# Sigmoid attention and two feed-forward layers on one core: GpSimd's additions and subtractions of weights and unit tiles are done by DVE and ACT

## The chip, the core and the metric

The kernel runs on one core of a Trainium2 chip. The core has a matrix engine (TensorE; in the rows PE, and PEld for its weight loads), VectorE (DVE), ScalarE (ACT), GpSimd (POOL), and SyncE (SP), which here issues nearly all transfers. Each engine works through its own instruction list in order; engines wait for each other on semaphores. The metric is device time in microseconds for one execution: the median of 3 runs of the kernel before is 1112.79 us (1111.52 to 1113.42).

## The reference

```python
# attention: 4 batches, 12 heads, 448 tokens, head size 64
scores = scale * q @ k.T - log(448)
attn = sigmoid(scores);  x = attn @ v            # -> [1792, 768]
# first layer, 1536 wide
xn = x / sqrt(mean(x * x) + 1e-6) * rms_g
g = xn @ w_gate;  val = xn @ w_val
x = (g * sigmoid(g) * val) @ w_out               # -> [1792, 768]
# second layer, 2048 wide
h = x @ w_in
out = (h - tanh(h)) @ w_out2                     # -> [1792, 768]
```

The weight matrices come as 64-bit numbers; everything else, and the result, is 32-bit.

## The kernel before, in words

All activations are kept transposed, in "unit" tiles of 128 x 448 (128 features of one batch's 448 tokens); there are 74 unit buffers. The products of both layers keep 32-bit accuracy by splitting each operand into a high part (a cast to fp32r, line 279) and a low part (the value less its high part: line 350 for weights, 595 and 635 for unit tiles); each product is then three matmuls (high by high, high by low, low by high).

The attention comes first, batch by batch. Then the two batches (0, 1) go through both layers, then the batches (2, 3). A layer has two kinds of jobs, and the jobs take turns:

- Jobs "Ag", "Av" (gate and value) and "C" (the second layer's input matrix) compute 2 x 2 blocks with seven products instead of eight (`seven_units`, matmuls on line 734). For that they need sums and differences of weight blocks (`total`, line 385) and of unit tiles (`right_sum`, line 600), each split again. Two or three products share one PSUM bank, and between them the bank is copied (line 279) or added to an earlier tile (`plus`, line 708). The next product in that bank can't start before that read. Behind them stand SiLU (678), the product of gate and value (681), tanh (685) and the subtraction (686); `parts` splits the results (279 and 635).
- Jobs "B" and "D" (the two output matrices) are ordinary products, six matmuls to a 128 x 128 weight block (line 769). Partial sums go to DRAM and come back.

Weights are prepared two jobs ahead (`conv`): for batches (0, 1) a 64-bit block is loaded, made into 32-bit values (`values32`: a cast on line 279 and one DVE instruction on line 339), summed (385), split (279 and 350), and the 32-bit values are written to DRAM (370); for batches (2, 3) they are read back (419) and split again.

The order of the instructions isn't written by hand. Each operation is given to `Plan.add` with the engines that can do it, a cost in nanoseconds for each, and a mark whether it uses the port that DVE and GpSimd share. `Plan.issue` then goes through the work with a clock for each engine: it takes, for each piece of work that is ready, the engine on which it starts soonest, and among the pieces that can start within 300 ns of the soonest the one that stands first in the program. The result is the fixed order on every engine. The costs are built by small functions: `act(n)`, `dve(n)`, `pool(n)` return a dictionary with one engine, and an operation that has a choice merges them, as on line 350:

```python
add({**dve(n, psum=False), **pool(n)}, lambda e: ENG[e].tensor_sub(lo(), of(), hi().bitcast(F32)), ...)
```

`pool(n)` is offered on lines 350 (low parts of weights), 385 (sums of weights), 538, 541 and 542 (squares for the norm, and their sum; there ACT or DVE took all of them), 595, 600 and 635 (unit tiles), and through line 675 on 681 and 686. The power on line 560 is given to GpSimd alone, with its own cost.

Of the kernel before, what the change touches and what calls it, by code (L numbers as in the profile page):

```python
# [214 lines left out]
def tile_sigmoid_attention_moe_moe(  # L215
# [37 lines left out]
    def slot(kind, pool, shape, dt, tag):  # L253
        return Slot(kind, lambda: pool.tile(shape, dt, tag=tag, name=tag))
# [18 lines left out]
        return {"DVE": ((150 if psum or fast else 210) + n / 0.96 / (2 if fast else 1), fast or (two and not psum))}  # L273

    def pool(n):
        return {"POOL": (230 + n * 2.16, True)}

    def copy(engines, to, of, reads, writes):
        add(engines, lambda e: (nc.scalar.copy if e == "ACT" else nc.vector.tensor_copy)(to(), of()), reads, writes)  # L279
# [68 lines left out]
    def split(n, hi, lo, of, reads, kh, kl):  # L348
        copy({**act(n), **dve(n, fast=True)}, hi, of, reads, [*kh])
        add({**dve(n, psum=False), **pool(n)}, lambda e: ENG[e].tensor_sub(lo(), of(), hi().bitcast(F32)), [*reads, *kh], [*kl])  # L350
# [21 lines left out]
    def conv(j):  # L372
# [11 lines left out]
        def total(to, n, x, y, sub=True):  # L384
            add({**dve(NH, psum=False), **pool(NH)}, lambda e: (ENG[e].tensor_sub if sub else ENG[e].tensor_add)(
                one_of(to.tile, n), one_of(x[0].tile, x[1]), one_of(y[0].tile, y[1])), [x[0][x[1]], y[0][y[1]]], [to[n]])
# [471 lines left out]
    for j in range(len(jobs)):  # L858
# [14 lines left out]
        if seven or tight == 1:  # L873
            n = 6 if seven else 2
# [75 lines left out]
```

## Time and profile before

| | |
|---|---|
| median of 3 runs | 1112.79 us |
| the profiled execution | 1111.01 us |
| its span, first to last instruction | 1109.2 us |
| TensorE busy | 1092.8 us (99%) |
| DVE busy | 701.0 us (63%), 1075 instructions |
| ACT busy | 503.2 us (45%), 896 instructions |
| GpSimd busy | 149.6 us (13%), 108 instructions |
| granted TensorE clock | 1.0 throughout |

The profiled execution took 1.8 us more than its span, which lies around the first and last instruction. It is itself 1.78 us below the median. Of the 108 instructions of GpSimd, 96 are the additions, subtractions and products of lines 350, 385, 595, 600, 635, 681 and 686, four are the powers of line 560, and the rest set constants. Busy time of the matmuls is modelled at their ends: a matmul's record is longer than the distance to the next one's start.

### The profile page before, as it was taken

To read this page: it belongs to the slowest core of one execution; us is meant where nothing else is said; L and a number is where in the kernel's file an instruction comes from. 1 tells how busy PE (TensorE), PEld (TensorE's weight loads), DVE (VectorE), ACT (ScalarE), POOL (GpSimd) and SP (SyncE) were. 2 spreads that over 40 slices of the span, in tenths; PEclk is the share of its full clock that TensorE was granted. 3 is DMA by queue.
4 is the path that set the end of the run, shared out by engine and by line. 5 is a ranking of instruction groups with operands and counts; after the bars stand their busy time and mean duration, and the time that the engine had idled before them with its cause. 6 is when DMAs were issued, how large, how long until landed. Compare 5 with 4: busy or idle time off the path is not lost.

```text
span 1109.2 us, 14723 instructions
## 1 busy us (share of the span) xinstructions
PE 1092.8 (99%) x5364; PEld 914.3 (82%) x5364; DVE 701.0 (63%) x1075; ACT 503.2 (45%) x896; POOL 149.6 (13%) x108
## 2 busy tenths in 40 slices
PE   9999999999999998999999999999999999999998
PEld 3333338999999997999998888999899989999997
DVE  0353816877478789767698966633666686474651
ACT  5776864443255346355364533312344353243431
POOL 0000003300021000123132001200021021222100
PEclk9999999999999999999999999999999999999999
DMA  5774554469668546599899563334344135656432
GB/s 163 246 221 114 143 177 179 146 253 316 212 207 282 208 157 232 181 321 364 288 345 320 192 198 119 115 121 135 103 164 147 57 103 159 195 179 199 146 116 100
DMA packets 92456, 211.40 MB, mean 191 GB/s; under 512 B 25312, under 2 KB 58080, under 8 KB 92384
## 3 DMA queue, kind: packets, MB, share of 16 engines
q1 hardware_dynamic: 92080, 210.30, 56.3%
q8 instruction: 42, 0.69, 0.3%
q14 instruction: 30, 0.25, 0.1%
q10 hardware_dynamic: 304, 0.16, 0.1%
HBM read 137.68 MB, written 72.74 MB: 190 GB/s over the span
## 4 chain that ended last, share of the span: by engine, by line
PE 94%; DVE 4%; issue 1%; ACT 1%; DMA 0%; POOL 0%; DVEq 0%; ACTq 0%; POOLq 0%
PE ps L734 42%; PE ps L769 37%; PE ps L490 7%; PE ps L520 7%; DVE unit L279 1%; DVE wt L350 1%; DVE unit L635 1%; PE ps L286 1%; DVE unit L708 0%; ACT unit L279 0%; DVE unit L681 0%; PE ps L554 0%; DMA wC<-cv 0%; ACT wt L279 0%; DVE unit L600 0%
## 5 line engine op out<-in xcount | busy, mean ns | idle before, releaser
L734 PE MATMUL ps<-unit,wt 128*128 128x448 f32 x2520 | 521.5, 366 | 9.6 <-DVE unit L708 5.4
L734 PEld LDWEIGHTS ps<-unit,wt 128*128 128x128 f32 x2520 | 471.4, 188 | 55.7 <-DVE unit L708 6.9
L769 PE MATMUL ps<-unit,wt 128*128 128x448 f32 x2016 | 413.9, 365 | 1.1 <-ACT wt L279 1.1
L769 PEld LDWEIGHTS ps<-unit,wt 128*128 128x128 f32 x2016 | 378.1, 188 | 33.1 <-ACT wt L279 1.5
L279 ACT COPY unit<-ps 128x448 f32<-128x448 f32 x172 | 91.2, 534 | 329.0 <-PE ps L769 200.5
L279 DVE COPY unit<-ps 128x448 f32<-128x448 f32 x80 | 49.9, 624 | 129.8 <-PE ps L769 124.0
L350 DVE TENSOR_TENSOR wt<-cv,wt 128x768 fp32r<-128x768 f32 (+1 forms) x111 | 101.7, 924 | 18.8 <-ACT wt L279 17.4
L279 ACT CAST wt<-cv 128x768 fp32r<-128x768 f32 (+1 forms) x97 | 75.1, 781 | 41.4 <-PE ps L734 16.3
L497 ACT ACTIVATE unit<-ps 128x448 f32<-128x448 f32 (+1 forms) x192 | 86.5, 547 | 5.9 <-PE ps L490 5.9
L635 DVE TENSOR_TENSOR unit<-unit 128x448 fp32r<-128x448 f32 x94 | 75.8, 807 | 7.4 <-ACT unit L279 4.7
L490 PE MATMUL ps<-wt 64*128 64x448 f32 (+1 forms) x384 | 78.9, 547 | 0.0
L520 PE MATMUL ps<-unit,vs 128*64 128x448 f32 (+1 forms) x384 | 77.7, 545 | 0.0
L350 POOL TENSOR_TENSOR wt<-cv,wt 128x768 fp32r<-128x768 f32 (+1 forms) x25 | 48.2, 1928 | 214.9 <-ACT wt L279 145.5
L708 DVE TENSOR_TENSOR unit<-ps,unit 128x448 f32<-128x448 f32 x84 | 51.9, 619 | 33.2 <-PE ps L734 23.7
L350 POOL TENSOR_TENSOR wt<-wt 128x768 fp32r<-128x768 f32 (+1 forms) x21 | 36.3, 1732 | 269.6 <-ACT wt L279 188.9
L279 ACT CAST wt<-wt 128x768 fp32r<-128x768 f32 (+1 forms) x60 | 44.8, 753 | 53.8 <-PE ps L734 38.0
L339 DVE SCALAR_TENSOR_TENSOR cv<-wt,zero 128x768 uint32<-128x768 uint32 x68 | 66.8, 982 | 2.5 <-ACT unit L535 0.7
L490 PEld LDWEIGHTS ps<-wt 64*128 64x128 f32 (+1 forms) x384 | 32.3, 173 | 43.3 <-issue 36.1
L520 PEld LDWEIGHTS ps<-unit,vs 128*64 128x64 f32 (+1 forms) x384 | 25.2, 136 | 49.1 <-issue 32.9
L279 ACT CAST zero<-wt 128x768 f16<-128x768 bf16 x49 | 53.1, 1083 | 26.6 <-DVE cv L339 19.8
L279 ACT CAST unit<-unit 128x448 fp32r<-128x448 f32 x91 | 51.3, 567 | 25.4 <-DVE unit L681 9.0
L350 DVE TENSOR_TENSOR wt<-wt 128x768 fp32r<-128x768 f32 (+1 forms) x59 | 51.4, 879 | 6.4 <-ACT wt L279 5.5
(49 smaller groups left out, 548.9 us busy)
## 6 DMA issues: line engine op xcount, KB each, us to landing
wt<-in_w_out SPq DMA_DIRECT2D x28, 768.0 KB, 5.9
sumD<-unit SPq DMA_DIRECT2D x72, 224.0 KB, 2.7
unit<-sumD SPq DMA_DIRECT2D x72, 224.0 KB, 4.7
wt<-in_w_in SPq DMA_DIRECT2D x16, 768.0 KB, 5.8
wC<-cv SPq DMA_DIRECT2D x32, 384.0 KB, 4.3
wt<-wC SPq DMA_DIRECT2D x16, 768.0 KB, 4.3
wt<-in_w_gate SPq DMA_DIRECT2D x12, 768.0 KB, 5.2
wt<-in_w_val SPq DMA_DIRECT2D x12, 768.0 KB, 5.4
```

What stands on the lines that cost most here:

```text
L279: add(engines, lambda e: (nc.scalar.copy if e == "ACT" else nc.vector.tensor_copy)(to(), of()), reads, writes)
L286: nc.tensor.matmul(ps[:, :S], lhsT=mark[:, :P], rhs=mark, start=True, stop=True)
L339: add(dve(NW, psum=False), lambda e: nc.vector.scalar_tensor_tensor(out=c.tile.bitcast(U32), in0=r.tile[:, :NW, 1], scalar=13, in1=z.tile, ...
L350: add({**dve(n, psum=False), **pool(n)}, lambda e: ENG[e].tensor_sub(lo(), of(), hi().bitcast(F32)), [*reads, *kh], [*kl])
L490: nc.tensor.matmul(ps[i, c].tile[:n, :S], lhsT=t.tile[rows, at:at + n], rhs=t.tile[rows, :S], start=True, stop=True)
L497: add(act(S, psum=True), lambda e: nc.scalar.activation(to.tile[at:at + n, :S], ps.tile[:n, :S], AF.Sigmoid, bias=-math.log(S), scale=1.0 ...
L520: nc.tensor.matmul(ps.tile[i * D:(i + 1) * D, :S], lhsT=v.tile[:n, c, i, :], rhs=a[c][i].tile[:n, :], start=(c == 0), stop=(c == 3))
L635: add({**pool(S), **dve(S, psum=False)}, lambda e: ENG[e].tensor_sub(c["l"].tile, t.tile, c["h"].tile.bitcast(F32)), [t["t"], kh], [kl])
L708: add(dve(S), lambda e: nc.vector.tensor_add(t.tile, ps.tile[:, :S], t.tile), [ps["t"], t["t"]], [t["t"]])
L734: nc.tensor.matmul(ps.tile[:, :S], lhsT=part(a), rhs=x[b].tile, start=n in ((1, 2, 5) if opening else (1, 5)) and i == 0 and q == 0, stop= ...
L769: nc.tensor.matmul(ps.tile[:, :S], lhsT=wt, rhs=a[p].tile, start=first and i == 0 and k < GR[ph], stop=last and i == 2, skip_group_check=True)
```

## The change

`pool(n)` returns an empty dictionary. Every operation that had it as one of two engines is left with the other one; line 560, which doesn't use the function, stays on GpSimd.

```diff
     def pool(n):
-        return {"POOL": (230 + n * 2.16, True)}
+        return {}
```

Since the planner's clocks change with it, the order on DVE and ACT changes from the first job of the first layer on. TensorE's order stays the same but for three matmuls beside the last norm. In the built program GpSimd keeps the constants and the four powers. DVE gets 96 more additions, subtractions and products: 46 of line 350 (41 of 128x768, five of 128x384), 24 of line 385, 18 of line 635, and 8 of lines 595, 600, 681 and 686. From DVE to ACT go 27 copies on line 279 between PSUM and unit tiles (unit<-ps from 80 to 66 on DVE, ps<-unit from 31 to 18); a few casts and copies go the other way.

Three places show it. The first is DVE where the first "C" job of batches (0, 1) opens: cv and wt are weight tiles, zero is the helper tile of `values32`, unit and ps the unit tiles and PSUM banks. Before:

```order
L339 SCALAR_TENSOR_TENSOR cv_3968<-wt_3721,zero_83 128x768
L350 TENSOR_TENSOR wt_3964<-cv_3949,wt_3964 128x768
L385 TENSOR_TENSOR cv_3974<-cv_3968 128x3x128
L385 TENSOR_TENSOR cv_3974<-cv_3974,cv_3949 128x3x128
L385 TENSOR_TENSOR cv_3949<-cv_3949,cv_3968 128x3x128
L385 TENSOR_TENSOR cv_3949<-cv_3949,cv_3974 128x3x128
L350 TENSOR_TENSOR wt_3989<-cv_3974,wt_3989 128x768
L350 TENSOR_TENSOR wt_4003<-cv_3949,wt_4003 128x768
L350 TENSOR_TENSOR wt_4008<-cv_3968,wt_4008 128x384
L708 TENSOR_TENSOR unit_3916<-ps_3897,unit_3916 128x448
L708 TENSOR_TENSOR unit_3970<-ps_3882,unit_3970 128x448
```

And in the changed kernel at the same place, up to the second of the two additions of line 708 (the first stands some places further ahead, between two weight operations):

```order
L350 TENSOR_TENSOR wt_3965<-cv_3950,wt_3965 128x768
L385 TENSOR_TENSOR cv_3977<-cv_3969 128x3x128
L385 TENSOR_TENSOR cv_3977<-cv_3977,cv_3950 128x3x128
L385 TENSOR_TENSOR cv_3950<-cv_3950,cv_3969 128x3x128
L385 TENSOR_TENSOR cv_3950<-cv_3950,cv_3977 128x3x128
L350 TENSOR_TENSOR wt_3992<-cv_3977,wt_3992 128x768
L350 TENSOR_TENSOR wt_4006<-cv_3950,wt_4006 128x768
L350 TENSOR_TENSOR wt_4011<-cv_3969,wt_4011 128x384
L686 TENSOR_TENSOR unit_3967<-unit_3920,unit_3967 128x448
L279 CAST unit_4018<-unit_3967 128x448
L635 TENSOR_TENSOR unit_4020<-unit_3967,unit_4018 128x448
L708 TENSOR_TENSOR unit_3973<-ps_3888,unit_3973 128x448
```

One addition of line 708 moved ahead of the weight work, and three unit operations moved in front of the other one.

The second place is DVE where the last "C" job of batches (0, 1) ends, beside the first unit tiles of batches (2, 3). Before:

```order
L686 TENSOR_TENSOR unit_5778<-ps_5719,unit_5778 128x448
L279 COPY unit_5801<-ps_5671 128x448
L635 TENSOR_TENSOR unit_5805<-unit_5778,unit_5799 128x448
L600 TENSOR_TENSOR unit_5813<-unit_5625,unit_5431 128x448
L279 CAST unit_5822<-unit_5813 128x448
L595 TENSOR_TENSOR unit_5827<-unit_5813,unit_5822 128x448
L708 TENSOR_TENSOR unit_5801<-ps_5715,unit_5801 128x448
L279 CAST unit_5849<-unit_5836 128x448
```

Now:

```order
L686 TENSOR_TENSOR unit_5778<-ps_5708,unit_5778 128x448
L279 CAST unit_5795<-unit_5778 128x448
L635 TENSOR_TENSOR unit_5807<-unit_5778,unit_5795 128x448
L595 TENSOR_TENSOR unit_5813<-unit_5766,unit_5780 128x448
L600 TENSOR_TENSOR unit_5820<-unit_5647,unit_5619 128x448
L279 CAST unit_5830<-unit_5820 128x448
L595 TENSOR_TENSOR unit_5834<-unit_5820,unit_5830 128x448
L708 TENSOR_TENSOR unit_5809<-ps_5704,unit_5809 128x448
```

The copy of the bank in front of line 708's addition left DVE (ACT does it), and a low part that GpSimd computed came in.

The third place is ACT where the first "C" job of batches (2, 3) opens; `ps_8137` is the bank that the next product waits for. Before:

```order
L279 CAST unit_8190<-unit_8143 128x448
L279 CAST wt_8213<-wt_7801 128x768
L279 CAST wt_8216<-wt_7801 128x384
L685 ACTIVATE unit_8221<-unit_8186 128x448
L279 COPY unit_8239<-ps_8137 128x448
```

Now:

```order
L279 CAST unit_8190<-unit_8143 128x448
L279 CAST wt_8213<-wt_7816 128x768
L279 CAST wt_8216<-wt_7816 128x384
L685 ACTIVATE unit_8219<-unit_8186 128x448
L279 COPY unit_8221<-ps_8137 128x448
L279 CAST wt_8238<-cv_7875 128x768
```

The copy of that bank after its sixth product, which DVE did before (`unit_8219`, straight behind its addition of line 708), is now on ACT, behind two casts of weights and a tanh. The copy that ACT had in this row before, of the same bank nine matmuls later, went to DVE.

## Rows read from the trace of the kernel before

**Rows 1.** The page: busy time, share of the span and instructions of each engine.

```profile
PE 1092.8 (99%) x5364; PEld 914.3 (82%) x5364; DVE 701.0 (63%) x1075; ACT 503.2 (45%) x896; POOL 149.6 (13%) x108
```

**Rows 2.** The page: matmul groups; busy us, mean ns | idle before, what ended it.

```profile
L734 PE MATMUL ps<-unit,wt 128*128 128x448 f32 x2520 | 521.5, 366 | 9.6 <-DVE unit L708 5.4
L769 PE MATMUL ps<-unit,wt 128*128 128x448 f32 x2016 | 413.9, 365 | 1.1 <-ACT wt L279 1.1
```

**Rows 3.** Groups of instructions on DVE and GpSimd, shapes apart; columns as in Rows 2.

```profile
L635 DVE TENSOR_TENSOR unit<-unit 128x448 fp32r<-128x448 f32 x94 | 75.8, 807 | 7.4 <-ACT unit L279 4.7
L595 DVE TENSOR_TENSOR unit<-unit 128x448 fp32r<-128x448 f32 x82 | 50.1, 622 | 4.3 <-ACT unit L279 2.6
...
L279 DVE CAST unit<-unit 128x448 fp32r<-128x448 f32 x105 | 48.4, 461 | 5.6 <-POOL unit L686 2.0
L350 POOL TENSOR_TENSOR wt<-cv,wt 128x768 fp32r<-128x768 f32 x24 | 47.2, 1966 | 209.8 <-ACT wt L279 140.4 <-DVE wt L279 55.4 <-DMA wC<-cv 13.9
...
L385 POOL TENSOR_TENSOR cv<-cv 128x384 f32<-128x384 f32 x24 | 29.1, 1212 | 184.6 <-DVE cv L385 82.7 <-DVE cv L339 48.0 <-DMA wAg<-cv 22.5
```

**Rows 4.** Windows of 50 us: busy PE, PEld, DVE, ACT, POOL, clock, DMA share, GB/s.

```profile
400.00:450.00 50.00, 45.11 (x216) 39.58 (x215) 44.77 (x73) 28.63 (x48) 3.21 (x3) 1.00 0.55 193
...
600.00:650.00 50.00, 46.55 (x225) 41.53 (x224) 45.10 (x77) 27.13 (x50) 5.63 (x4) 1.00 0.72 239
```

**Rows 5.** Timeline near 360 us: start, us, what [idle before it, releaser].

```profile
359.62 1.86 POOL L350 TENSOR_TENSOR wt<-cv,wt 128x768 fp32r<-128x768 f32 x1 [16.81 <-ACT wt L279]
...
360.33 1.40 DVE L279 CAST unit<-unit 128x448 fp32r<-128x448 f32 x1
...
362.98 2.32 PE L734 MATMUL ps<-unit,wt 128*128 128x448 f32 x10 [0.28 <-DVE unit L279]
```

**Rows 6.** Timeline of 668 to 676 us; the PE rows from TensorE's own.

```profile
668.73 1.85 POOL L350 TENSOR_TENSOR wt<-wt 128x768 fp32r<-128x768 f32 x1 [18.02 <-ACT wt L279]
668.86 2.20 DVE L635 TENSOR_TENSOR unit<-unit 128x448 fp32r<-128x448 f32 x1
...
673.26 0.95 DVE L350 TENSOR_TENSOR wt<-wt 128x768 fp32r<-128x768 f32 x1
...
675.60 40.66 PE L734 MATMUL ps<-unit,wt 128*128 128x448 f32 x198 [0.62 <-ACT unit L279]
...
796.83 40.38 PE L734 MATMUL ps<-unit,wt 128*128 128x448 f32 x198 [0.57 <-ACT unit L279]
```

**Rows 7.** Timeline of 605 to 626 us.

```profile
605.47 1.56 POOL L600 TENSOR_TENSOR unit<-unit 128x448 f32<-128x448 f32 x1
...
605.93 1.58 DVE L600 TENSOR_TENSOR unit<-unit 128x448 f32<-128x448 f32 x1
...
609.19 2.08 PE L734 MATMUL ps<-unit,wt 128*128 128x448 f32 x9 [1.52 <-DVE unit L708]
...
624.95 0.83 ACT L279 CAST wt<-cv 128x768 fp32r<-128x768 f32 x1
...
625.84 15.00 PE L769 MATMUL ps<-unit,wt 128*128 128x448 f32 x72 [1.15 <-ACT wt L279]
```

**Rows 8.** Timeline of 417 to 442 us: TensorE, and one DVE row.

```profile
417.90 2.82 PE L734 MATMUL ps<-unit,wt 128*128 128x448 f32 x11 [0.62 <-ACT unit L279]
...
421.08 2.21 DVE L385 TENSOR_TENSOR cv<-cv 128x384 f32<-128x384 f32 x4
...
426.86 13.13 PE L734 MATMUL ps<-unit,wt 128*128 128x448 f32 x63 [2.14 <-DVE unit L708]
441.59 9.39 PE L734 MATMUL ps<-unit,wt 128*128 128x448 f32 x45 [1.60 <-DVE unit L708]
```

**Rows 9.** Timeline of 892 to 894 us.

```profile
892.54 1.25 ACT L279 CAST wt<-wt 128x768 fp32r<-128x768 f32 x2 [2.35 <-PE ps L734]
893.22 27.62 PE L734 MATMUL ps<-unit,wt 128*128 128x448 f32 x135 [0.72 <-DVE unit L279]
...
893.70 0.58 ACT L685 ACTIVATE unit<-unit 128x448 f32<-128x448 f32 x1
```

## The prediction, made before the changed kernel ran

> **What bounds the kernel now.** I read the page's busy times first, then the groups of matmuls with what ended their idle time, then the 50 us windows, then the timeline at each place where TensorE waited. The reader is to see four things. TensorE is busy 1092.8 of 1109.2 us, GpSimd only 149.6 [rows 1]. Of the 16.4 us in which TensorE stands still, the two matmul groups of the layers have 9.6 and 1.1 us [rows 2]; the rest lies at the start and behind the last matmul, where no GpSimd arithmetic stands. So 10.7 us is what any change on the other engines can give, and a little more: a matmul's record is 366 ns long [rows 2] while 198 of them take 40.66 us, 205 ns each [rows 6], so each wait costs some 0.16 us more than the idle time that is shown. Twelve waits make 2 us: the bound on the gain is about 12.7 us, 1.1%. There is no such bound on the loss.
>
> Third, the waits sit at a few places: the two stretches in which DVE is nearly full (44.77 and 45.10 us of 50 [rows 4]), where a "C" job or the second pair of batches opens, and single waits near 363, 676, 797 and 893 us. Fourth, in several of them DVE was held up by GpSimd: a cast of a unit tile took 1.40 us beside a GpSimd subtraction [rows 5], line 635 took 2.20 us beside another [rows 6], line 600 1.58 us beside GpSimd's own line 600 [rows 7]. The same form of instruction on line 595 takes 0.62 us [rows 3].
>
> **The change: what moves.** GpSimd loses 96 instructions, and DVE gets them all. On DVE they cost: 41 of line 350 at 0.95 us [rows 6], 39 us; five half as wide, some 2.8 us; 24 of line 385 at 2.21 / 4 = 0.55 us [rows 8], 13 us; 26 on unit tiles at 0.62 us [rows 3], 16 us. That is 71 us, against 47.2 us that GpSimd needed for 24 instructions of line 350 alone and 29.1 us for line 385 [rows 3]. Against this stands what DVE no longer loses beside GpSimd: line 635 averaged 807 ns against 622 ns for the same form on line 595, over 94 instructions 17.4 us [rows 3]; the casts and the other lines have some more of it, which I put at 8 us (an estimate: the 105 casts average 461 ns [rows 3], with instances such as the 1.40 us of rows 5 among them). And 27 copies go to ACT, 17 us at 0.62. So DVE goes from 701 to 701 + 71 - 17 - 8 - 17 = 730 us (66%), ACT from 503 to about 510. Neither becomes a bound over the span. What counts is each place where TensorE waits. All other moved work I cost at nothing: it lies beside the 4536 matmuls of the layers, which have 10.7 us of idle time before them in all [rows 2]; if that cover were gone at one place, an instruction of line 350 there costs 0.95 us.
>
> **Place by place** (idle time shown plus 0.16 us for each wait).
>
> (a) 363 us. The cast that ended only behind GpSimd's instruction (359.62 + 1.86 = 361.48) stands ahead of the bank copy for which TensorE waited 0.28 us [rows 5]. DVE's order is the same in the changed kernel, without GpSimd: -0.4 us.
>
> (b) 676 and 797 us, the same pattern twice. Line 635 ends 1.6 us late behind GpSimd, so do the next ones and line 350 at 673.26; ACT's cast waits for it, and the copy that TensorE needs stands behind that cast. TensorE waits 0.62 and 0.57 us [rows 6]. The ACT order stays, the GpSimd instruction goes: -1.5 us for both. At the lock itself the Trainium skill (SBUF — State Buffer, Who interferes with whom) says that a DVE instruction with two SBUF inputs and a GpSimd instruction that reads SBUF exclude each other, the second blocked until the first ends; the 2.20 us beside a GpSimd instruction of 1.85 us agree. By that rule 1.6 us of DVE time come back at each place, 3.2 us in all; by the wait rows only 0.62 and 0.57 us of it reached TensorE, and these are taken.
>
> (c) 605 to 626 us. TensorE waited 1.52 us for line 708, which stood behind line 600, held for 0.96 us [rows 7]. Now nothing holds it, and the bank copy ahead of it is on ACT, but a low part (0.62 us) that GpSimd had stands in its place. Between 0.96 and 1.68 us come back; I take 1.3. Of that 0.5 are lost again some 40 matmuls later, since one more low part and a weight subtraction stand ahead of the low parts that the next job needs. The wait of 1.15 us at 625.84 was for a cast on ACT [rows 7] that stood behind a copy; in the new order the cast stands ahead of that copy, so 1.3 come back. Sum -2.1 us, bounds 0 and -3.0.
>
> (d) 418 to 442 us, four waits, the two last 2.14 and 1.60 us [rows 8], all behind DVE, which is full. In the new row the second addition of line 708 has three unit operations more ahead of it (0.62 + 0.46 + 0.62 = 1.7 us, means of rows 3) and a cast of weights that ACT had (below ACT's 0.83 us [rows 7]); it has the first addition less (0.62), and two low parts that stood between weight instructions now stand before all of them (up to 1.2). Up to the next wait two more sums (1.1 us [rows 8]) come in, and the unit operations done earlier drop out. Ends: -1.0 (the wait shrinks, because DVE comes into the row further ahead) and +2.7 (everything added is paid). DVE has the same work but for the cast and the sums, so I take +0.7, nearer the lower end.
>
> (e) 893 us. TensorE waited 0.72 us for a bank copy that DVE did straight away [rows 9]. In the new order ACT does it, behind two weight casts and a tanh. ACT's casts began at 892.54; 1.25 us for both, then 0.58 for the tanh and 0.53 for a copy, less some 0.2 us by which neighbours overlap, ends it at 894.7 instead of 893.2: +1.5 us. Ends +0.9 and +1.6: the three instructions ahead can't be passed.
>
> Sum: -0.4 - 1.5 - 2.1 + 0.7 + 1.5 = -1.8 us. Against the profiled execution that is 1111.0 - 1.8 = 1109.2 us; this execution lay 1.78 us below the median, so against the median of the runs 1112.8 - 1.8 = **1111.0 us**, 0.16% less. A measurement of this kernel can tell about 0.2%, 2.2 us, from no change.
>
> **Rivals.**
>
> *More comes back (1107.7 us).* DVE comes into the crowded stretches further ahead, since nothing blocks it before. Then (d) ends at its lower end, -1.0, (c) at -3.0, and (e) at +0.9: -0.4 - 1.5 - 3.0 - 1.0 + 0.9 = -5.0. For it speaks that one addition of line 708 moved ahead of the weight work; against it that the new row of (d) is no shorter.
>
> *DVE overflows (slower, 1117.1 us).* In the two stretches where DVE has some 5 us of 50 free, GpSimd did 3.21 and 5.63 us of work [rows 4], on DVE about half, 4.4 us. If the queue in front of TensorE's releasers grows by it, (d) pays +2.7, (c) gains nothing, (e) costs 1.6, and (a) and (b) are lost again at the next wait: +4.3. It decides from the point where DVE, at the opening of the "C" job, is still at weights when line 708 is due. The Trainium skill (Perfetto Trace Analysis, Optimizing Scalar/DVE Operations) speaks for it: with DVE saturated, handing work to ACT or even GpSimd may pay, which this change takes back; it adds that between GpSimd and DVE, which share a port, it might not help. The 45.10 us of 50 agree with a saturated stretch, the 63% of the span don't.
>
> *Nothing to be told (1112.8 us).* The blocked time wasn't what TensorE waited for: each wait is followed by another cause that is as late, and the openings weigh (a) to (c) up. For it speaks that of the 17 us of blocking on line 635 alone only some 3 us were seen in TensorE's waits.
>
> That GpSimd keeps the work is excluded by the built order.
>
> **How the numbers follow.** Forecast 0.48, its own range 1109 to 1113.5 (faster 0.18, same 0.29, slower 0.01, since it lies near the edge of 0.2%). More comes back 0.20, all faster. DVE overflows 0.18 (slower 0.17, same 0.01). Nothing 0.14 (same 0.11, faster 0.02, slower 0.01). Faster 0.40, same 0.41, slower 0.19. The range reaches to the first rival and most of the way to the second: 1107.5 to 1115.5.
>
> **What would show it.** In the new profile GpSimd has four powers and constants; DVE is busy 720 to 740 us; line 635 on DVE averages below 640 ns, and no DVE instruction on unit tiles takes over 1 us. TensorE's waits near 363, 676 and 797 us are gone, that for line 708 near 608 us is below 0.9 us, that near 893 us is above 2 us and ends with ACT instead of DVE; the four waits from 418 us on sum to 5 to 6.5 us. Wrong would be: the wait at 893 unchanged (then (e) fails), DVE instructions as long as before without GpSimd (then the lock was not the cause), or new waits for weight subtractions of line 350 in stretches that had none, which is the second rival.

## The result, and the profile after

The changed kernel takes 1117.88 us (median of 6 runs, 1115.87 to 1120.70), the kernel before beside it 1112.79 us (6 runs): a ratio of 1.0051, interval 1.0031 to 1.0071. It is slower, and outside the range of the forecast. The profiled execution took 1119.03 us, its span is 1117.2 us against 1109.2. The 1112.79 us for the kernel before lie high: in the 87 runs of it beside the experiments the medians are 1110.80 to 1111.28 us, and against those the changed kernel loses more (1.0065, e5 below).

The page of the changed kernel: busy times, then three groups (busy us, mean ns | idle before, releaser).

```profile
PE 1098.2 (98%) x5364; PEld 918.2 (82%) x5364; DVE 718.9 (64%) x1158; ACT 508.0 (45%) x909; POOL 6.2 (1%) x12
...
L734 PE MATMUL ps<-unit,wt 128*128 128x448 f32 x2520 | 525.7, 368 | 12.7 <-ACT unit L279 7.6
...
L769 PE MATMUL ps<-unit,wt 128*128 128x448 f32 x2016 | 416.0, 366 | 0.6 <-DVE unit L279 0.6
...
L635 DVE TENSOR_TENSOR unit<-unit 128x448 fp32r<-128x448 f32 x112 | 69.9, 624 | 9.0 <-ACT unit L279 5.8
```

GpSimd is nearly empty, and DVE is not crowded over the span: 718.9 us, less than the 730 of the forecast. Line 635 went from 807 to 624 ns [rows 3]. But TensorE itself is busy 5.4 us longer with the same 5364 matmuls [rows 1], and its idle time in the two groups is 13.3 us instead of 10.7 [rows 2]. So more time went into longer matmuls than into waits.

TensorE's timeline in the changed kernel, at its three longest waits (the rows of 598, 611 and 612 us stand beside the second).

```profile
426.73 14.66 PE L734 MATMUL ps<-unit,wt 128*128 128x448 f32 x63 [3.21 <-DVE unit L708]
...
598.40 6.58 PE L734 MATMUL ps<-unit,wt 128*128 128x448 f32 x30
608.18 3.02 PE L734 MATMUL ps<-unit,wt 128*128 128x448 f32 x9 [3.20 <-ACT unit L279]
611.00 2.05 PE L769 MATMUL ps<-unit,wt 128*128 128x448 f32 x6
612.89 3.82 PE L734 MATMUL ps<-unit,wt 128*128 128x448 f32 x18
...
899.17 29.30 PE L734 MATMUL ps<-unit,wt 128*128 128x448 f32 x135 [2.23 <-ACT unit L279]
```

The first and the third are waits of before that have grown: 2.14 us became 3.21 [rows 8], 0.72 became 2.23 [rows 9]. The second is new. The last "C" job of batches (0, 1) runs its products in the order 1, 5, 6, 2, 7, 4, 3, nine matmuls each, and the wait stands ahead of product 7, for the copy of the bank after product 6. In the kernel before TensorE passed this place without a stop:

```profile
596.21 8.40 PE L734 MATMUL ps<-unit,wt 128*128 128x448 f32 x39
```

The 1.52 us for line 708 [rows 7], ahead of product 3, are gone: products 4 and 3 are the 18 matmuls at 612.89, without a stop.

And the same 63 matmuls that took 13.13 us [rows 8] now take 14.66; nine at 608 us take 3.02 us, where nine of the same form took 2.08 [rows 7]. Windows of the changed kernel behind these waits show why; the column before the last two is the granted clock.

```profile
428.00:431.00 3.00, 3.00 (x11) 2.64 (x10) 2.82 (x5) 2.18 (x3) 0.00 (x0) 0.52 0.63 154
...
432.00:434.00 2.00, 2.00 (x11) 1.83 (x11) 1.12 (x3) 0.00 (x0) 0.00 (x0) 1.00 0.97 364
609.00:612.00 3.00, 3.00 (x10) 2.65 (x9) 2.26 (x5) 2.27 (x5) 0.00 (x0) 0.50 1.02 401
...
899.00:902.00 3.00, 2.83 (x8) 2.53 (x9) 1.75 (x4) 0.95 (x2) 0.00 (x0) 0.53 0.29 121
```

Behind each of the three waits the granted clock falls to 0.50, the 1.2 GHz level, and 8 to 11 matmuls start in 3 us instead of 15; then it is back at 1.00. The Trainium skill (TensorE: Matmul & The Clock Gate, Part 1) has the same two levels and says that "the default state is throttled, and activity releases the throttle"; the windows agree on the two levels. In the kernel before the clock was 1.00 in the same stretches.

Where each microsecond went can be read from the starts of the same groups of matmuls in the two timelines (changed minus before):

| place | before | changed | difference | step since the row above |
|---|---|---|---|---|
| L769, 210 matmuls | 366.74 | 365.79 | -0.95 | -0.95 |
| L769 behind the first C job | 450.82 | 451.97 | +1.15 | +2.10 |
| L769, 132 matmuls | 512.15 | 514.16 | +2.01 | +0.86 |
| L734 ahead of the second pair | 640.67 | 645.86 | +5.19 | +3.18 |
| L769 after 676 us | 716.10 | 720.38 | +4.28 | -0.91 |
| L734, 36 matmuls | 884.75 | 889.14 | +4.39 | +0.11 |
| L769 after 893 us | 920.68 | 928.30 | +7.62 | +3.23 |
| last L769, 138 matmuls | 1077.16 | 1085.20 | +8.04 | +0.42 |

The step of +0.86 up to 512 us is another wait that the kernel before did not have:

```profile
496.95 11.26 PE L734 MATMUL ps<-unit,wt 128*128 128x448 f32 x54 [0.95 <-ACT unit L279]
```

### The profile page after: what moved, and what is told of

It is laid out like the page before. It is cut to its first block, busy times and chain, and to the rows that moved or that the text cites. A ratio compares the mean times of both kernels' runs of the same rounds, so it can differ in the third digit from the quotient of the medians.

```text
span 1117.2 us, 14596 instructions
## 1 busy us (share of the span) xinstructions
PE 1098.2 (98%) x5364; PEld 918.2 (82%) x5364; DVE 718.9 (64%) x1158; ACT 508.0 (45%) x909; POOL 6.2 (1%) x12
## 4 chain that ended last, share of the span: by engine, by line
PE 89%; DMA 4%; DVE 4%; ACT 2%; issue 1%; SPq 0%; POOL 0%; DVEq 0%; ACTq 0%; POOLq 0%
PE ps L734 41%; PE ps L769 34%; PE ps L490 7%; PE ps L520 7%; DMA wC<-cv 1%; DVE wt L350 1%; ACT unit L279 1%; DMA unit<-sumD 1%; DMA wAv<-cv 1%; DMA wAg<-cv 1%; DMA wt<-in_w_out 1%; PE ps L286 0%; DMA unit<-x 0%; ACT wt L279 0%; DVE cv L339 0%
## 5 line engine op out<-in xcount | busy, mean ns | idle before, releaser
L734 PE MATMUL ps<-unit,wt 128*128 128x448 f32 x2520 | 525.7, 368 | 12.7 <-ACT unit L279 7.6
L734 PEld LDWEIGHTS ps<-unit,wt 128*128 128x128 f32 x2520 | 474.8, 189 | 59.2 <-ACT unit L279 11.1
L769 PE MATMUL ps<-unit,wt 128*128 128x448 f32 x2016 | 416.0, 366 | 0.6 <-DVE unit L279 0.6
L769 PEld LDWEIGHTS ps<-unit,wt 128*128 128x128 f32 x2016 | 378.8, 188 | 34.1 <-DVE unit L279 1.0
L279 ACT COPY unit<-ps 128x448 f32<-128x448 f32 x186 | 98.3, 534 | 356.4 <-PE ps L769 207.0
L350 DVE TENSOR_TENSOR wt<-cv,wt 128x768 fp32r<-128x768 f32 (+1 forms) x136 | 120.8, 895 | 10.4 <-ACT wt L279 9.0
L279 DVE COPY unit<-ps 128x448 f32<-128x448 f32 x66 | 41.2, 624 | 122.1 <-PE ps L769 119.4
L635 DVE TENSOR_TENSOR unit<-unit 128x448 fp32r<-128x448 f32 x112 | 69.9, 624 | 9.0 <-ACT unit L279 5.8
L350 DVE TENSOR_TENSOR wt<-wt 128x768 fp32r<-128x768 f32 x80 | 67.8, 855 | 8.2 <-ACT wt L279 6.7
L279 ACT CAST zero<-wt 128x768 f16<-128x768 bf16 x47 | 50.6, 1076 | 19.1 <-DVE cv L339 11.4
L542 DVE TENSOR_TENSOR unit<-unit 128x448 f32<-128x448 f32 x20 | 12.5, 623 | 65.6 <-ACT unit L535 65.5
L595 DVE TENSOR_TENSOR unit<-unit 128x448 fp32r<-128x448 f32 x84 | 51.2, 622 | 4.3 <-ACT unit L279 2.2
L385 DVE TENSOR_TENSOR cv<-cv 128x384 f32<-128x384 f32 x80 | 43.0, 554 | 16.8 <-DMA wAg<-cv 8.7
```

The source lines that it names most:

```text
L595: add({**pool(S), **dve(S, psum=False)}, lambda e: ENG[e].tensor_sub(t["l"].tile, of.tile, t["h"].tile.bitcast(F32)), [of["t"], kh], [kl])
L635: add({**pool(S), **dve(S, psum=False)}, lambda e: ENG[e].tensor_sub(c["l"].tile, t.tile, c["h"].tile.bitcast(F32)), [t["t"], kh], [kl])
L734: nc.tensor.matmul(ps.tile[:, :S], lhsT=part(a), rhs=x[b].tile, start=n in ((1, 2, 5) if opening else (1, 5)) and i == 0 and q == 0, stop= ...
L769: nc.tensor.matmul(ps.tile[:, :S], lhsT=wt, rhs=a[p].tile, start=first and i == 0 and k < GR[ph], stop=last and i == 2, skip_group_check=True)
```

## Experiments

My theory after the result: the change itself gives back what the waits near 363 and 676 us cost; it lost because the planner ordered DVE, ACT and SP anew and made three waits of over 2 us, each followed by a clock fall that costs about as much again. The rivals: only the idle time counts; or the amount of work on DVE and ACT is too much.

### Is it the clock? (e3, e4, e1, e5)

e3 makes one wait of the kernel before longer: three copies of a tile onto itself on DVE, ahead of line 708 in the first C job.

```diff
+            def run(e):
+                if x == "z" and (ph, bs, p) == ("C", (0, 1), 0) and not late:
+                    late.append(1)
+                    for _ in range(3):
+                        nc.vector.tensor_copy(t.tile, t.tile)
+                nc.vector.tensor_add(t.tile, ps.tile[:, :S], t.tile)
```

> The kernel before with three copies of a unit tile onto itself ahead of one addition of line 708, the one for which TensorE waits 2.14 us at 426.9 us; they lengthen that wait to about 3.3 us and change no value. Theory (the clock): the longer wait makes the granted clock fall to 0.50 behind it: +1.2 us of wait and +1.6 us of slow matmuls, 1112.8 + 2.8 = 1115.6 us. Rival (only the idle time counts): 1114.0 us, clock at 1.00 in the stretch behind it.

e4 adds matmuls of zeros in front of that wait, by a table of places (e1 has the same lines and two more places):

```diff
+FILL = {("C", (0, 1), 0, 4, 2): (("x", 15),)}
...
+                for x_, count in FILL.get((ph, bs, p, n, i), ()):
+                    for _ in range(count):
+                        nc.tensor.matmul(banks[x_].tile[:, :S], lhsT=mark[:, :P], rhs=mark, start=False, ...)
```

> The same as the kernel before with the three added copies, and 15 matmuls of zeros ahead of the wait that they lengthen. Theory (the clock): no fall, so only the longer stop counts, 1112.8 + 1.2 = 1114.0 us, clock at 1.00. Rival (only the idle time counts): the same 1114.0 us here, and no difference to the kernel without the zeros.

e3: 1114.15 us (8 runs), ratio 1.0029, 1.0018 to 1.0039; e4: 1112.47 us (11 runs), 1.0008, 1.0000 to 1.0017; the kernel before beside both 1111.28 us (18 runs). TensorE's timeline of e3 and a window of it:

```profile
427.61 14.65 PE L742 MATMUL ps<-unit,wt 128*128 128x448 f32 x63 [3.44 <-DVE unit L714]
```

```profile
429.00:430.00 1.00, 1.00 (x4) 0.92 (x3) 0.89 (x2) 1.00 (x2) 0.00 (x0) 0.50 0.76 287
```

And of e4:

```profile
423.39 3.01 PE L744 MATMUL ps<-mark 128*128 128x448 bf16 x15
...
427.59 13.14 PE L746 MATMUL ps<-unit,wt 128*128 128x448 f32 x63 [0.58 <-DVE unit L715]
```

The waiting matmul starts at 427.6 us in both; DVE does the same in both. Only the 63 matmuls behind differ, 14.65 against 13.14 us, and the medians by 1.7 us. That is the price of one fall, shown by itself. Both medians are as the clock theory had them against the kernel before (+2.9 and +1.2 us, forecast +2.8 and +1.2).

e1 fills the three waits of the changed kernel. e5 is the changed kernel once more.

> The changed kernel with 41 matmuls of zeros onto zeros, added to open sums (so they change no value), in TensorE's queue right ahead of the three long waits (15 at 426.7 us, 15 at 608.2 us, 11 at 899.2 us); every other engine has the same instructions in the same order. Theory (the clock): the loss is mostly that TensorE's granted clock falls to 0.50 for some 3.4 us behind each of the waits of 3.21, 3.20 and 2.23 us; with TensorE at work in them the clock stays at 1.00, the copies end when they did, and about 1.6 us come back at each place: 1117.9 - 5 = 1113 us, mean clock .998 or more. Rival (the waits themselves and the later work they push back are the loss): the time stays at 1117.5 to 1118.5 us. Second rival (the added matmuls cost their own time): 1118 to 1120 us.

> The changed kernel once more, so that the three kernels beside it are compared with it on one chip: 1116 to 1119 us, mean clock .994 to .998, three waits of over 2 us (near 427, 608 and 899 us).

e5: 1118.89 us (6 runs), ratio 1.0065, 1.0051 to 1.0078. e1: 1115.14 us (5 runs), ratio 1.0034, 1.0021 to 1.0047, with a mean clock of .999 or 1.000 in every run. Timeline of e1:

```profile
427.48 13.14 PE L742 MATMUL ps<-unit,wt 128*128 128x448 f32 x63 [0.35 <-DVE unit L713]
...
607.38 2.08 PE L742 MATMUL ps<-unit,wt 128*128 128x448 f32 x9 [1.59 <-ACT unit L284]
...
896.89 27.65 PE L742 MATMUL ps<-unit,wt 128*128 128x448 f32 x135
```

No fall is left: the 63, 9 and 135 matmuls take 13.14, 2.08 and 27.65 us instead of 14.66, 3.02 and 29.30. From the first group of the table to the last the profile is 4.7 us shorter than that of the changed kernel. The ratios say 1.9 and 3.4 us (against either measurement of the changed kernel), less than the 5 that I expected. Not every run of the changed kernel can have all its falls, for the mean clocks of its runs go from .998 to .994; that this makes the difference is argued. So e1 misses its 1113 us, and 3.8 us of the loss against the kernel before (1.0034) are left with the clock at 1.00: they are not the clock, but the waits, with whatever the added matmuls cost. In the profile of e5 the clock did not fall at the third place, though the wait was the same:

```profile
427.50 15.62 PE L734 MATMUL ps<-unit,wt 128*128 128x448 f32 x63 [3.22 <-DVE unit L708]
...
901.41 27.66 PE L734 MATMUL ps<-unit,wt 128*128 128x448 f32 x135 [2.23 <-ACT unit L279]
```

### What makes the wait near 608 us? (e6, e9)

ACT's timeline in the changed kernel, ahead of the copy for which TensorE waits (607.60):

```profile
601.55 0.54 ACT L279 COPY ps<-unit 128x448 f32<-128x448 f32 x1 [0.91 <-DMA unit<-sumD]
604.48 1.06 ACT L279 CAST zero<-wt 128x768 f16<-128x768 bf16 x1 [2.39 <-DMA wt<-in_w_out]
607.13 0.54 ACT L279 COPY ps<-unit 128x448 f32<-128x448 f32 x1 [1.59 <-DMA unit<-sumD]
607.60 0.53 ACT L279 COPY unit<-ps 128x448 f32<-128x448 f32 x1
```

And in the kernel before:

```profile
597.80 1.67 ACT L279 COPY ps<-unit 128x448 f32<-128x448 f32 x3
...
600.65 0.54 ACT L279 COPY ps<-unit 128x448 f32<-128x448 f32 x1 [0.44 <-DMA unit<-sumD]
601.12 0.53 ACT L279 COPY unit<-ps 128x448 f32<-128x448 f32 x1
```

The copy is on ACT in both kernels. ACT takes its instructions in order; TensorE's copy stands behind copies of reloaded sums into banks, five of them before and three now, and now behind a cast for a weight that is not needed yet. e6 moves that cast back, by telling the planner that loads land later:

```diff
-                out=flat(r.tile)[:, 1:4 * NW + 1], in_=flat(src)), [], [r["t"]], after=2000)
+                out=flat(r.tile)[:, 1:4 * NW + 1], in_=flat(src)), [], [r["t"]], after=5500)
```

> The changed kernel with one number of the planner changed: a load of weights is reckoned to land 5.5 us after its issue instead of 2.0, so that work which needs it is queued later. By the built order the cast of the weight that waited for its load on ACT ahead of a bank copy (608 us) then stands behind that copy. Theory (ACT's queue behind a transfer caused that wait, and the clock fall doubles it): the wait of 3.20 us near 608 us shrinks below 1 us, no fall there; 2.4 us of wait and 1.6 us of clock come back, 4 us less than the changed kernel beside it; the waits near 427 and 899 us with their falls stay. Rival (only the idle time counts): 2.4 us less. Second rival (the wait was DVE's or the load itself is late): no change, the wait stays.

1117.39 us (6 runs), ratio 1.0058, 1.0042 to 1.0073, against 1.0065 for e5: no difference that can be told. My reading was wrong in one link. ACT in e6:

```profile
607.68 0.54 ACT L279 COPY ps<-unit 128x448 f32<-128x448 f32 x1 [5.59 <-DMA unit<-sumD]
608.15 0.53 ACT L279 COPY unit<-ps 128x448 f32<-128x448 f32 x1
```

The cast is gone from there, and ACT waits 5.59 us for the reload of a sum instead; TensorE's wait is 2.72 us. So the reload is what comes last. e9 ranks the loads of weights lower in the planner:

```diff
     def load(j):
...
+        plan.later += 30
...
+        plan.later -= 30
```

> The changed kernel with the loads of weights ranked 30 places later, so that SP issues the load of a w_out block (597.28 us in the changed kernel) behind the reloads of the partial sums instead of ahead of them. Theory (the wait near 608 us is for those reloads: they stand behind a load of 768 KB in a stretch in which the DMA engines are full, and the copy that TensorE needs stands behind them on ACT): the wait of 3.2 to 4.0 us near 608 us shrinks to 0.5 to 1.2 us; 2.5 us of wait and 1 to 2 us of clock come back, 3 to 4.5 us less than the changed kernel, 1114 to 1116 us. Rival (ACT's order alone makes the wait): it stays at 2.5 us or more and the time at 1117 to 1119 us.

1112.79 us (12 runs), ratio 1.0020, 1.0009 to 1.0030: 5 us less than e5 by the ratios, a little more than forecast. The waits near 427 and 899 us are still there in its profile (3.19 and 2.23 us). TensorE's wait at the place is 1.15 us, and the clock stays at 1.00 there:

```profile
606.99 2.10 PE L736 MATMUL ps<-unit,wt 128*128 128x448 f32 x9 [1.15 <-ACT unit L279]
```

SP's queue in e9, then in the changed kernel, then in the kernel before:

```profile
593.72 0.42 SPq L646 DMA_DIRECT2D unit<-sumD  x1
...
595.01 0.43 SPq L646 DMA_DIRECT2D unit<-sumD  x1
596.99 0.33 SPq L330 DMA_DIRECT2D wt<-in_w_out  x1
...
598.32 2.92 SPq L646 DMA_DIRECT2D unit<-sumD  x4
```

```profile
596.16 1.03 SPq L644 DMA_DIRECT2D unit<-sumD  x2
597.28 0.41 SPq L329 DMA_DIRECT2D wt<-in_w_out  x1
...
599.68 2.63 SPq L644 DMA_DIRECT2D unit<-sumD  x3
...
604.42 0.32 SPq L644 DMA_DIRECT2D unit<-sumD  x1
```

```profile
595.58 2.02 SPq L644 DMA_DIRECT2D unit<-sumD  x4
...
601.02 2.10 SPq L329 DMA_DIRECT2D wt<-in_w_out  x2
```

ACT's last copy ahead of TensorE's needs the third reload of this stretch. In the kernel before it is the first of the four from 595.58 us on, and the loads of w_out come behind it. In the changed kernel it is the first of the three from 599.68 us on, behind a load of w_out at 597.28: 4.1 us later, where TensorE itself is 2.2 us later (598.40 against 596.21 us), and ACT could use it only at 607.13 us. In e9 the load still stands ahead of four reloads, so the wording of my expectation did not come true; but the first five reloads are issued 1.4 to 2.4 us earlier, and the copy follows. The stretch is one in which the DMA engines are full, in the changed kernel (the column ahead of the last is their share):

```profile
600.00:606.00 6.00, 4.98 (x25) 4.29 (x23) 5.31 (x12) 2.22 (x4) 0.00 (x0) 1.00 1.00 345
```

In the kernel before the share was 0.80 in the same six us. Which of the other transfers delays them most in the changed kernel stays open.

### Which half of the change? (e7, e8)

e7 takes only the weights off GpSimd, e8 only the unit tiles.

```diff
     def pool(n):
-        return {}
+        return {"POOL": (230 + n * 2.16, True)}
-        add({**dve(n, psum=False), **pool(n)}, ...     # e7: lines 350 and 385 without GpSimd
+        add({**dve(n, psum=False)}, ...
-        add({**pool(S), **dve(S, psum=False)}, ...     # e8: all uses of pool(S) without it
+        add({**dve(S, psum=False)}, ...
```

> One half of the change: only the weights' additions and subtractions (lines 350 and 385) leave GpSimd, those of unit tiles may stay on it. Theory (the weights carry the loss, since they put 52 us on DVE and ACT's queue is reordered around them): the long waits near 608 and 899 us are there as in the changed kernel, one in the first C job is longer than 2 us too, three falls: 1116 to 1119 us. Rival (the unit tiles carry it): near the kernel before, 1112 to 1114 us.

> The other half: only the work on unit tiles leaves GpSimd, the weights may stay on it. Theory (the weights carry the loss at 608 and 899 us, the unit tiles ahead of line 708 that at 427 us): one long wait of 3 to 3.5 us near 427 us with one fall, none near 608 and 899 us: 1.2 us of wait and 1.6 us of clock over the kernel before, 1114 to 1115.5 us. Rival (the unit tiles carry all of it): 1116 to 1119 us with three falls.

e7: 1116.99 us (5 runs), ratio 1.0051, 1.0039 to 1.0063, as forecast, with falls at 443, 608 and 898 us. e8: 1117.27 us (5 runs), ratio 1.0046, 1.0033 to 1.0059; forecast 1114 to 1115.5, so missed. Each half loses about as much as the whole; by the amount of work the halves would add up to it. e7, TensorE:

```profile
427.12 13.12 PE L734 MATMUL ps<-unit,wt 128*128 128x448 f32 x63 [2.11 <-DVE unit L708]
443.18 10.96 PE L734 MATMUL ps<-unit,wt 128*128 128x448 f32 x45 [2.95 <-DVE unit L708]
608.03 3.43 PE L734 MATMUL ps<-unit,wt 128*128 128x448 f32 x9 [2.85 <-ACT unit L279]
897.95 29.17 PE L734 MATMUL ps<-unit,wt 128*128 128x448 f32 x135 [2.23 <-ACT unit L279]
```

And e8:

```profile
426.77 14.69 PE L734 MATMUL ps<-unit,wt 128*128 128x448 f32 x63 [2.11 <-DVE unit L708]
607.40 2.62 PE L734 MATMUL ps<-unit,wt 128*128 128x448 f32 x9 [3.69 <-ACT unit L279]
901.11 27.66 PE L734 MATMUL ps<-unit,wt 128*128 128x448 f32 x135 [0.72 <-DVE unit L279]
```

The wait at 899 us belongs to the weights: with them on GpSimd the copy is on DVE and waits 0.72 us. The wait at 608 us comes with either half. And the same wait of 2.11 us at 427 us is followed by a fall in e8 (14.69 us) and by none in e7 (13.12).

### Undoing the copy at 899 us (e2)

```diff
+            ways = dve(S) if (ph, bs, p, n) == ("C", (2, 3), 0, 6) else {**act(S, psum=True), **dve(S)}
```

> The changed kernel with one bank copy, that after the sixth product of the first C job of batches 2 and 3 (the one for which TensorE waits 2.23 us at 899 us), kept on DVE as before the change. Theory (the clock): the wait goes back to about 0.7 us, -1.5 us, and the clock does not fall behind it, another -1.6 us: 3.1 us less than the changed kernel, about 1114.8 us. Rival (only the idle time counts): -1.5 us, 1116.4 us. Both fail if DVE's copy is late there too.

1121.47 us (4 runs), ratio 1.0091, 1.0077 to 1.0105: the wrong way. TensorE and DVE in e2:

```profile
901.47 29.98 PE L735 MATMUL ps<-unit,wt 128*128 128x448 f32 x135 [4.43 <-DVE unit L279]
```

```profile
897.94 0.96 DVE L350 TENSOR_TENSOR wt<-wt 128x768 fp32r<-128x768 f32 x1 [0.85 <-ACT wt L279]
...
900.80 0.62 DVE L279 COPY unit<-ps 128x448 f32<-128x448 f32 x1
```

Forced onto DVE, the copy was queued behind a weight subtraction that GpSimd had (at 893.51 us, 1.84 us long, in the kernel before) and four more instructions; on ACT it began at 898.60 in the changed kernel. So the planner's choice of ACT was the better one: on both engines work is queued ahead of the copy, the weights' most of all (e13 below puts the copy ahead of a part of it).

### Order or amount? (e10 to e16)

Three settings change what the planner chooses and no computation: SOON (how long an engine is kept for work of a better rank), the rank of what follows a product (lines 703 and 708), and the rank of the loads.

```diff
-SOON = 300
+SOON = 120        # 100 in e10 and e11
...
             if i == 2:
+                plan.later -= 20     # e12 to e15
                 done(n)
+                plan.later += 20
...
+        plan.later += 60             # in load(), e14 to e16
```

> The changed kernel with the planner's constant SOON at 100 ns instead of 300: it keeps an engine waiting for work of a better rank for less long, and so orders DVE's and ACT's queues anew everywhere. Theory (the change lost by three crowded places in the order, not by DVE's or ACT's load): with another order of the same work, in which by the built program no bank copy stands behind more than two instructions at these places, no wait is above 2 us, the clock stays at .999 or more, and the time is at the kernel before or below, 1106 to 1112 us. Rival (the load of 719 us on DVE is itself too much): waits of 2 us and more stay in the crowded stretches, 1115 us or more.

> The kernel before, with GpSimd's work on GpSimd, and the same SOON of 100 ns. Theory: the order matters more than GpSimd; this kernel is at 1107 to 1112 us too, and within 3 us of the changed kernel with the same constant. Rival (GpSimd's work off it is what counts): the changed kernel with this constant is faster by more than 3 us.

> The kernel before with SOON at 120 ns and the copies and additions behind a product (lines 703 and 708 and what follows them) ranked 20 places earlier. Theory (TensorE waits for bank copies that stand behind other work): the waits of 2.14 and 1.60 us in the first C job go, the waits of the layers sum to 5 to 7 us instead of 10.7, the clock stays at 1.00: 1105 to 1109 us. Rival (ranks only move the waits): 1110 to 1113 us.

> The changed kernel with the same two settings as the kernel before that did best (SOON at 120 ns, the copies and additions behind a product ranked 20 places earlier): the change alone, under another order. Theory (the loss is order, and the load ahead of the reloads is one part of it): the waits at 427 and 443 us are gone, that near 606 us is still 2 to 5 us with its fall: 1109 to 1112 us, 2 to 5 us over the kernel before with these settings. Rival (GpSimd's work on DVE and ACT costs by its amount): 5 us or more over it, in waits that the kernel before does not have.

> The same with the loads of weights ranked 60 places later, so that they stand behind the reloads of the sums. Theory: the wait near 606 us falls below 1.2 us, no wait of the layers is above 1.2 us, the clock stays at .999 or more: 1104 to 1108 us, below the kernel before as it was, so that the change is then no loss. Rival (DVE's 719 us are too much): 1110 us or more.

> The kernel before, GpSimd's work on GpSimd, with the three settings of the kernel beside it. Theory (what GpSimd does is worth the 2 us that the waits near 363, 676 and 797 us show, no more): 1104 to 1109 us, within 3 us of the changed kernel with the same settings. Rival (moving the work off GpSimd is a loss whatever the order): more than 3 us faster than the changed kernel with the same settings.

> The changed kernel with SOON at 120 ns and the loads ranked 60 places later, without the rank of the copies. Theory: only the wait near 894 us (1.6 us for the copy behind two weight casts on ACT) is above 1 us, and no fall: 1105 to 1108 us. Rival: a wait of over 2 us near 606 us with a fall, 1110 us or more.

Medians, and ratios to the unaltered kernel before on the same chip:

| order | GpSimd's work on GpSimd | off it |
|---|---|---|
| as it was | 1 | 1.0051 and 1.0065 |
| SOON 100 | e11: 1109.65, 0.9984 (0.9972 to 0.9996) | e10: 1112.81, 1.0014 (1.0005 to 1.0022) |
| SOON 120, copies ranked | e12: 1107.37, 0.9967 (0.9954 to 0.9979) | e13: 1109.40, 0.9982 (0.9974 to 0.9991) |
| the same, loads ranked | e15: 1114.52, 1.0024 (1.0015 to 1.0032) | e14: 1109.82, 0.9985 (0.9976 to 0.9993) |
| SOON 120, loads ranked | not run | e16: 1107.27, 0.9958 (0.9946 to 0.9970) |

With the same work off GpSimd the time goes from 1118.9 to 1107.3 us by the planner's choices alone. Against the kernel before under the same settings the change loses 5.7 to 7.2 us in the first row, loses 3.3 and 1.7 us in the next two, and gains 4.3 us in the fourth, by the ratios; but that gain comes from a wait of e15 in the attention (below), which no setting aimed at. So these runs show that the choices of the planner move the time by more than the change does; a price of the change by itself they don't show. The best on each side, e12 and e16, beat both given kernels, and which of the two is faster can't be told.

One rival is not quite out. The settings change not only the order but also who does what: in e10, e13, e14 and e16 DVE is busy 696 to 701 us instead of 719, since ACT took casts of unit tiles (in e16 DVE has 55 of them instead of 109). All additions and subtractions that left GpSimd are still on DVE there. No run is as fast as the kernel before with 719 us on DVE; the nearest is e9, 719.4 us at 1.0020. So most of the loss is not DVE's amount of work, and the last 0.2% may be.

The misses: e10 kept one long wait, and it is the one for the reloads,

```profile
606.05 3.73 PE L734 MATMUL ps<-unit,wt 128*128 128x448 f32 x9 [5.10 <-ACT unit L279]
```

with the waits at 427 and 443 us gone, as forecast. e11 is 3.3 us under e10, where I had allowed 3. e14 still waited 2.26 us near 605 us in its profile (forecast below 1.2) and lies above its forecast. e15 missed by 5 us: its profile has a wait of 3.78 us up to 175.55 us, in the attention, with the clock at 0.50 from 175 to 180 us. The times of e12, e13 and e16 came out as forecast; the waits of e12's layers sum to 3.7 us, less than the 5 to 7 forecast, and e13 is 1.7 us over e12 by the ratios, under the 2 to 5. e13 settles the wait at 899 us: with the copy ranked ahead of the second weight cast and the tanh it is 0.75 us, on ACT. e16 has no long wait left and a clock of 1.000 in each of its 5 runs:

```profile
422.23 27.76 PE L736 MATMUL ps<-unit,wt 128*128 128x448 f32 x135 [0.62 <-ACT unit L279]
605.04 3.90 PE L736 MATMUL ps<-unit,wt 128*128 128x448 f32 x18 [0.49 <-ACT unit L279]
889.08 27.84 PE L736 MATMUL ps<-unit,wt 128*128 128x448 f32 x135 [1.63 <-ACT unit L279]
```

In it SP issues the reloads from 590 to 595 us, six us earlier than in the changed kernel, and ACT does four copies into banks in a row at 596.76 without a wait.

## Why the prediction was wrong

The bound on the gain, 12.7 us, was not reached by any run (e16 gains 4.7 us by the ratios). The DVE tally was 11 us too high (718.9 us instead of 730, just under the 720 to 740 named as a sign). The other signs that were named came true: line 635 fell to 624 ns, the waits at 363, 676 and 797 us and that for line 708 near 608 us are gone, that at 893 us ended with ACT at 2.23 us, the four waits from 418 us on are in their range. The time still went the other way. By its steps, with the table of starts:

- (a), forecast -0.4: the wait is gone, and 0.95 us were won by 366 us, more than forecast.
- (b), -1.5 for both: the waits at 676 and 797 us are gone, TensorE runs 324 and 360 matmuls there without a stop. Of the two, 0.9 us show in the table at the first; at the second the step is +0.11, since the 210 matmuls of line 769 behind the first took 43.31 us against 42.50; why is open.
- (d), +0.7: the four waits sum to 5.44 us (0.62, 0.35, 3.21, 1.26), within the 5 to 6.5 forecast. The step in the table is +2.1: the fall behind the 3.21 us makes 1.5 of it.
- (e), +1.5: the wait went from 0.72 to 2.23 us, ending with ACT behind the two casts and the tanh, as worked out. The table has +3.2: again the fall, 1.6.
- (c), -2.1, is the step that failed: it came out at +3.2. Its own two waits did what it said: 1.52 us became none and 1.15 us became 0.60. What it left out is a wait that was not there before: 3.20 us for the copy after product 6, with 1.6 us of slow matmuls behind it. The step went over the waits that the trace of before shows, and "All other moved work I cost at nothing" covered the rest. But this copy is not moved work, it was on ACT before; it became late because the last reload ahead of it in ACT's queue is issued 4.1 us later by SP and lands late. 3.20 + 1.6 - 1.52 - 0.55 is 2.7 of the 3.2 us. The prediction never read SP's queue at this place, though the reloads and their landing are in the trace of before. The 0.95 us at 497 us is a second wait that is new and was costed at nothing.

The second failure is not a step but a price that ran through all of them: "each wait costs some 0.16 us more than the idle time that is shown". That was read from short waits. Behind a wait of 3.2 us it is 1.6 us more, or 2.5 (15.62 against 13.13 us in e5). With 1.5 or 1.6 us on (c), (d) and (e) the prediction's sum would have risen by 4.7 us; (c) without its fall makes another 3.7 (3.2 - 1.6 + 2.1). -1.8 + 4.7 + 3.7 is 6.6 of the 8.0 us by which the two profiles differ.

The rival "DVE overflows" named a time, 1117.1 us, close to the result, but that is luck: what was added ahead of line 708 at 427 us were unit operations, not weights, (a) was not lost again, the wait of (c) was for ACT and not for DVE, and some 4.7 us of the profile's 8.0 are falls of the clock, which it did not have.

## What to carry to other kernels

Where a planner sets the order, a change of which engine may do what changes every queue. Going through the waits of the old trace is not enough, for the longest new one here stood where there was none. Before pricing the moved work, follow what TensorE needs through all in-order queues back to SP, with each DMA that an instruction ahead of it waits for. Price a wait like those here at its length and, beyond that, at the matmuls that may then run at half clock (1.5 to 2.5 us here). And when the moved work seems to cost more than its amount, try another order before giving the change up.

## What was unexpected of the hardware

In these runs a stop of TensorE of 2.1 to 3.2 us was followed by half clock in some executions and not in others: near 427 us in e8 and not in e7 (2.11 us each), near 899 us in the changed kernel and not in e5 (2.23 us each), at 427 us in the changed kernel and not in the profile of e2 (3.21 us each; 13.14 us for the 63 matmuls there). So a kernel that waits that long spreads: the changed kernel's six runs go from 1115.87 us at a mean clock of .997 to 1120.70 at .994. Of the 29 runs of the kernel before beside e9 to e12, seven had .998 and took 1112.65 to 1113.92 us, the others 1110.30 to 1111.47; that its wait of 2.14 us [rows 8] is where those seven lost it is argued, no profile of such a run was taken. Matmuls of zeros in TensorE's queue kept the clock at 1.00 through a stop that other engines made.
